# A quarter of the second chunk's projections moved beside the first's, and a rarely taken branch kept to two engines

## The chip, the core and the metric

The kernel runs on one core of a Trainium2 chip. A core has five engines with instruction streams of their own: TensorE (PE, matrix products; PEld is its loading of weights), VectorE (DVE), ScalarE (ACT), GpSimd (POOL) and SyncE (SP), which here only issues DMAs. They wait for each other through semaphores. Data is in DRAM, in the on-chip SBUF (128 partitions), and in eight PSUM banks of 128 x 512 floats, into which PE writes. The metric is the device time of one execution in microseconds (us). A number such as L325 is a line of the kernel before.

## What is computed

The reference has two independent parts, whose results are concatenated:

```python
# part A: S = 2048 rows, D = 448 columns, 16 heads of 28, one key and one value for all heads
q = (x @ wq) in heads;  k = x @ wk;  v = x @ wv
p = softmax(q k^T * 28 ** -0.5)
a = concat_heads(p v) @ wo
# part B: a filter in the frequency domain
X = rfft2(x) * (w_r + 1j * w_i)
b = irfft2(X)
out = concatenate([a, b], axis=-1)
```

All of it is in 32-bit floats. Many products are made from a high and a low part of each factor (`wqh` and `wql`, `xh` and `xl`): the high part is a rounded copy in the format that PE reads fast, the low part is the rest, and three matmuls (high x high, low x high, high x low) give the product.

The softmax is taken with a shift per query that is estimated before the scores are known: a bound from the largest entries of q and k. If the bound is too wide (over `BOUND`), a block of code computes the exact row maxima instead. With this input the block is not entered.

## The kernel before

**Projections.** q, k and v are one product of x (transposed, four chunks of 512 rows, `c`) with a weight matrix of four groups of 128 columns (`g`). The 448 inner terms are cut into four quarters (`j`), 128 rows each; the last quarter has 64 rows twice, so that high and low part of x lie over each other and two matmuls do. `proj` (L321) issues the matmuls of one group and quarter, in the order (wqh, xh), (wql, xh), (wqh, xl). For chunk 0 the loop goes over quarters outside and groups inside (L351), into four PSUM banks, so that work starts with the first data; for chunks 1 to 3 it goes over groups outside (L375), one bank after the other.

**The first loads.** `raw` (L282) takes one of eight buffers and issues a load. All the loads of x and of the weights stand in SP's queue: x quarter 0 of chunk 0, the weights' quarter 0 in two pieces (columns 0 to 127 and the rest), then x and weights of quarters 1 to 3 in turn. `split_w` (L303) makes wqh on ACT and wql on DVE; `split_x` (L310) makes xh (on DVE for chunk 0, on ACT for the others) and xl on DVE. Before that PE runs 20 products of zeros (`WARM`, L277).

**Banks.** Six PSUM banks are in a ring, `free`, and `bank()` (L224) takes the next one. The two others, tags `aux` and `po`, are used by the second DFT step of part B (`fft1_mm`) in the meantime.

**The DFTs** of part B are worked in between: `fft1_*` for the first DFT in eight parts (results `bs` stored to a DRAM tensor `t1` by SP), later `fft2_*` and `fft3_*`. The copies `bs` of part 6 and 7 are on DVE.

**The end of the projections.** From L418 on, the first query tile `qa` (called `qf` there) is put together by ACT, DVE and DMAs, the bound is computed on DVE (`bits`, L435), PE does the last DFT parts and transposes the values (L445, into `pv`), and PE issues the first four score products into banks `a, b, d, f` (L453, `first_scores`). Then all five engines load `bits` from SBUF into a register (L458) and branch on it (L459). The block inside uses PE and DVE in a loop of 64 turns and at its end has the first scores again. After it ACT copies the last DFT part (`pa7`), DVE copies `pv` to `vs`, and `keys(1)` makes the second half of the keys.

**The main stage** is a list of 256 steps (`PLAN`, L46). Each step has four scores (L783), whose exp ACT takes (L786), and 16 products with vs (L758), four for each score, issued later. Units of the DFTs (A, B, Z, F) and of the output projection (W) stand between the scores at places written in the plan. PE issues in that order, by hand; from L502 on DVE's order is the program's too. A score takes the first bank of `free` and gives it back after its exp; step 0 used the four scores that were already there. The first unit A (`fft2_a`) needs `b`, which SP loads from `t1` (L550) and DVE splits (L567, L568).

Of the kernel before, what the change touches and what calls it, by code (L numbers as in the profile page):

```python
# [10 lines left out]
F32 = mybir.dt.float32  # L11
# [45 lines left out]
def kernel(ctx: ExitStack, tc: tile.TileContext, t: dict):  # L57
# [174 lines left out]
    with tc.tile_pool(name="w1", bufs=1) as w1:  # L232
# [37 lines left out]
        with tc.tile_pool(name="x1", bufs=2) as x1:  # L270
# [6 lines left out]
            for n in WARM:  # L277
                nothing = bank()
                for _ in range(n):
                    mm(nothing[:, :256], idle[:, :128], idle, start=True, stop=True)  # L280

# [39 lines left out]
            def proj(pq, xh, xl, g, j):  # L321
                gs = slice(g * 128, (g + 1) * 128)
                parts = ((wqh, xh), (wql, xh), (wqh, xl)) if j < 3 else ((wqh, xh), (wql, xh))
                for n, (w, x) in enumerate(parts):
                    mm(pq, w[:, j, gs], x[:, j], start=(j == 0 and n == 0), stop=(j == 3 and n == 1))  # L325
# [120 lines left out]
        fft1_out(6, pb6, bound)  # L446

        d, f, a, b, e, c = free
        begin = a, b, d, f

        def first_scores():
            for n, s in enumerate(begin):
                mm(s, ka[:, :128], qf[:, n], start=True, stop=True)  # L453

        first_scores()


        rv = nc.values_load(bits.bitcast(I32)[0:1, 0:1])  # L458
        with tc.If(rv > int(np.float32(BOUND).view(np.int32))), tc.tile_pool(name="g1", bufs=1) as g1:  # L459
            k4 = g1.tile([128, S], F32, name="k4")  # L460
            nc.vector.memset(k4, 0.0)
            for i in range(4):
                nc.vector.tensor_copy(k4[32 * i:32 * i + DH], kf[0:DH])
            mz = g1.tile([128, 4, 32], F32, name="mz")
            nc.vector.memset(mz, 0.0)


            qv = qraw.rearrange("p g (b q) -> p (g b) q", q=128)
            banks = a, b
            with tc.For_i(0, 64, 1) as n:  # L470
                qs = g1.tile([128, 128], F32, name="qs")
                nc.vector.tensor_copy(qs, qv[:, bass.ds(n, 1)][:, 0])
                mx = g1.tile([128, 4, 4], F32, name="mx")
                for i in range(4):
                    r = slice(32 * i, 32 * i + 32)
                    for h in range(4):
                        ps = banks[0]
                        mm(ps, qs[r], k4[r, h * 512:(h + 1) * 512], start=True, stop=True)
                        nc.vector.tensor_reduce(mx[:, i, h:h + 1], ps, axis=AX.X, op=ALU.max)
                nc.vector.tensor_reduce(mz[:, :, DH], mx, axis=AX.X, op=ALU.max)  # L480
                pt = banks[1][:, :128]
                mm(pt, mz.rearrange("p i d -> p (i d)"), ident, start=True, stop=True)
                nc.vector.scalar_tensor_tensor(qs, qs, mask, pt, op0=ALU.mult, op1=ALU.add)
                nc.vector.tensor_copy(qv[:, bass.ds(n, 1)][:, 0], qs)
# [459 lines left out]
```

## Time and profile before

| | |
|---|---|
| time, median of 3 runs | 654.41 us (654.33 to 655.7) |
| the profiled execution: its own time | 654.11 us |
| its span, first instruction to last | 652.3 us |
| PE, ACT, DVE, POOL busy | 645.8, 555.2, 360.8, 60.0 us |
| granted TensorE clock, mean | 0.999 |
| moved by DMA | 62.40 MB, mean 96 GB/s |

How to read it: the span lies inside the execution's time, some 1.8 us of which are around it. Matmuls are pipelined and their ends are modelled, so one after the other starts well before the former's end as shown; the distance of two starts says more than the length. Rows of a timeline have the start, the length, the engine, the line, the operation, the tiles written and read, and in brackets how long the engine had been idle and what ended that. An engine with a q (DVEq, PEldq) is its sequencer, which issues the instructions.

### The profile page before, as it was taken

The numbers are of one execution on the slowest core, as the hardware profiler recorded it, in microseconds if no ns is written. First come the engines' busy times: TensorE is split into PE (matmuls) and PEld (weight loads), VectorE is DVE, ScalarE is ACT, GpSimd is POOL, SyncE is SP. The second block draws the span as 40 slices with busy tenths as digits, with TensorE's granted clock in tenths as the row PEclk, the third lists the DMA queues.
The fourth block names the chain that finished last, engine by engine and source line by source line (L and its number), as shares of the span: only waits on it lengthen the run. The fifth ranks groups of instructions, "written<-read, shape, count | busy, mean of one in ns | idle before, by whom it ended". The sixth has DMA issues, their size and how long they took to land.

```text
span 652.3 us, 11930 instructions
## 1 busy us (share of the span) xinstructions
PE 645.8 (99%) x4480; PEld 378.6 (58%) x4480; DVE 360.8 (55%) x810; ACT 555.2 (85%) x1100; POOL 60.0 (9%) x111
## 2 busy tenths in 40 slices
PE   8999999999999999999999999999999999999997
PEld 6877645545545565555546565555555565565655
DVE  5999636776788732778652511356353510356533
ACT  4554899999999977999999987899999987899991
POOL 3021401101011000100010100010010100010010
PEclk9999999999999999999999999999999999999999
DMA  8756963434354123412061403131232313140001
GB/s 263 267 150 168 256 172 86 122 86 123 105 136 136 42 52 93 115 53 58 28 160 37 110 15 92 43 100 40 70 84 66 103 31 91 44 109 16 14 30 58
DMA packets 34380, 62.40 MB, mean 96 GB/s; under 512 B 6657, under 2 KB 22674, under 8 KB 33356
## 3 DMA queue, kind: packets, MB, share of 16 engines
q1 hardware_dynamic: 30448, 49.21, 26.9%
q0 software_dynamic: 3296, 11.49, 6.8%
q8 instruction: 36, 0.59, 0.4%
q10 hardware_dynamic: 576, 0.92, 0.4%
q14 instruction: 24, 0.20, 0.1%
HBM read 29.35 MB, written 14.75 MB: 68 GB/s over the span
## 4 chain that ended last, share of the span: by engine, by line
PE 88%; ACT 0%; ACTq 0%; issue 0%
PE s L783 30%; PE s L758 22%; PE sx L758 9%; PE po L783 5%; PE po L758 4%; PE s L678 4%; PE sx L783 4%; PE s L641 2%; PE s L629 1%; PE po L678 1%; PE s L538 1%; PE s L539 1%; PE s L537 1%; PE sx L629 0%; PE sx L678 0%; ACT yb L683 0%
## 5 line engine op out<-in xcount | busy, mean ns | idle before, releaser
L786 ACT ACTIVATE p<-s 128x512 f32<-128x512 f32 x795 | 430.2, 651 | 42.1 <-PE s L783 41.0
L783 PE MATMUL s<-qa,ka 128*128 128x512 f32 x791 | 245.9, 407 | 0.0
L783 PEld LDWEIGHTS s<-qa,ka 128*128 128x128 f32 x791 | 142.7, 188 | 86.3 <-ACT p L786 50.5
L758 PE MATMUL s<-p,vs 128*32 128x512 f32 x1280 | 149.3, 596 | 0.0
L758 PEld LDWEIGHTS s<-p,vs 128*32 128x32 f32 x1280 | 36.2, 109 | 81.4 <-issue 78.9
L786 ACT ACTIVATE p<-po 128x512 f32<-128x512 f32 x124 | 80.2, 647 | 3.5 <-PE po L783 3.4
L786 ACT ACTIVATE p<-sx 128x512 f32<-128x512 f32 x105 | 69.1, 658 | 4.1 <-PE sx L783 4.0
L666 DVE RECIPROCAL r<-r 128x128 f32<-128x128 f32 x64 | 61.0, 953 | 2.3
L758 PE MATMUL sx<-p,vs 128*32 128x512 f32 x512 | 59.6, 596 | 0.0
L783 PE MATMUL po<-qa,ka 128*128 128x512 f32 x124 | 50.5, 407 | 0.0
L783 PE MATMUL sx<-qa,ka 128*128 128x512 f32 x105 | 42.0, 400 | 0.0
L685 DVE COPY ya<-s 128x448 f32<-128x448 f32 x9 | 5.6, 624 | 56.1 <-PE s L678 56.1
L649 POOL TENSOR_TENSOR yo<-y 128x226 f32<-128x226 f32 x16 | 10.0, 622 | 273.7 <-issue 248.4
L758 PEld LDWEIGHTS sx<-p,vs 128*32 128x32 f32 x512 | 14.5, 109 | 32.8 <-issue 31.4
L758 PE MATMUL po<-p,vs 128*32 128x512 f32 x256 | 29.9, 596 | 0.0
L783 PEld LDWEIGHTS po<-qa,ka 128*128 128x128 f32 x124 | 23.4, 188 | 10.8 <-ACT p L786 7.0
L643 DVE COPY m<-s 128x452 f32<-128x452 f32 x14 | 8.8, 628 | 33.8 <-PE s L641 33.8
L631 DVE COPY z<-s 113x512 f32<-113x512 f32 (+1 forms) x11 | 7.6, 691 | 35.4 <-PE s L629 30.5
L325 PE MATMUL s<-xh,wqh 128*128 128x512 f32 x64 | 26.1, 408 | 0.8 <-ACT wqh L307 0.8
L325 PE MATMUL s<-xh,wql 128*128 128x512 f32 x64 | 25.4, 397 | 0.3 <-DVE wql L308 0.2
L783 PEld LDWEIGHTS sx<-qa,ka 128*128 128x128 f32 x105 | 19.7, 188 | 8.8 <-ACT p L786 3.5
L329 ACT ACTIVATE qraw<-s 128x512 f32<-128x512 f32 x16 | 9.3, 600 | 18.0 <-PE s L325 18.0
(188 smaller groups left out, 726.6 us busy)
## 6 DMA issues: line engine op xcount, KB each, us to landing
qa<-qa SPq DMA_DIRECT2D x15, 512.0 KB
raw<-xa SPq DMA_DIRECT2D x16, 256.0 KB, 5.5
xb<-xb SPq DMA_DIRECT2D x8, 512.0 KB, 3.5
qa<-qh SPq DMA_DIRECT2D x64, 64.0 KB, 2.0
qa<-ql SPq DMA_DIRECT2D x60, 64.0 KB, 2.0
ob<-yo SPq DMA_DIRECT2D x16, 226.0 KB, 2.2
t<-bs SPq DMA_DIRECT2D x16, 225.0 KB, 3.4
wr<-wr POOLq DMA_DIRECT2D x16, 225.0 KB, 3.8
```

Source lines behind the costliest of these rows:

```text
L325: mm(pq, w[:, j, gs], x[:, j], start=(j == 0 and n == 0), stop=(j == 3 and n == 1))
L329: out = nc.scalar.activation(qraw[:, g, cs], pq, AF.Copy)
L537: mm(out, fc[w + "h"], h, start=True, stop=False)
L631: nc.vector.tensor_copy(z[:w], pz[:w].rearrange("p j (r n) -> p r j n", r=2))
L641: mm(py[:, k], z[:w, r, js], cs3[:w, k], start=True, stop=True)
L643: nc.vector.tensor_copy(m, py)
L649: nc.gpsimd.tensor_tensor(yo[:, 0:2], y1[:, 0], y1[:, 1], op=ALU.add)
L666: nc.vector.reciprocal(r, r)
L678: mm(p, x[c][:, g, s], w[:, g], start=(g == 0 and n == 0), stop=(g == NG - 1 and n == 2))
L758: mm(po[c, g][32 * i:32 * i + 32], vs[:, kc], ps[i // 2][:, i % 2], start=(kc == 0), stop=(kc == 15))
L783: begun.append(mm(sc, ka[:, kc * 128:(kc + 1) * 128], qa[c, g][:, n], start=True, stop=True))
L786: nc.scalar.activation(ps[-1][:, n % 2], sc, AF.Exp, scale=SCALE)
```

## The change

Three things are changed.

- x quarter 0 of chunk 1 is loaded third, after the weights' quarter 0 and before x quarter 1 of chunk 0. Its 12 products (four groups, three each) are issued right after those of chunk 0's quarter 0. Chunk 1's four sums are therefore open while chunk 0's are: their banks are `aux`, `po` and two of the ring, and all eight banks are in use. `parts_of(1)` comes earlier; chunk 1 later does quarters 1 to 3 only. The first load for chunk 2 is issued behind the first loads of the DFT.
- Inside `proj` the order is (wqh, xh), (wqh, xl), (wql, xh). In quarter 0 of chunk 0 the groups 1 to 3 first do the two products with wqh, all three groups, and then those with wql. Two more products of zeros stand behind group 0.
- The value load and the branch are for DVE and POOL alone, and stand ahead of the two copies `fft1_out(6, ...)`, which now come after the block. The block is written for these engines: keys are spread over the partitions by DMA through DRAM, and products and maxima are made on DVE, without loops (8 x 4 x 64 turns of three instructions each). The first four scores are no longer issued ahead of the branch: step 0 issues its own, like every other, and the ring starts as `a, b, d, e, f, c`.

```diff
@@ -274,10 +274,14 @@
             nc.vector.memset(idle, 0.0)
-            for n in WARM:
+
+            def zeros(n):
                 nothing = bank()
                 for _ in range(n):
                     mm(nothing[:, :256], idle[:, :128], idle, start=True, stop=True)
+
+            for n in WARM:
+                zeros(n)
@@ -291,6 +295,8 @@
                 nc.sync.dma_start(wr[0][:, s], t["wq"][:, 0, s])
+
+            xr[1, 0] = raw(t["xa"][1, :, 0], nc.sync)
             for j in range(1, NK):
@@ -318,11 +324,13 @@
-            def proj(pq, xh, xl, g, j):
+            def proj(pq, xh, xl, g, j, some=(0, 1, 2)):
+
                 gs = slice(g * 128, (g + 1) * 128)
-                parts = ((wqh, xh), (wql, xh), (wqh, xl)) if j < 3 else ((wqh, xh), (wql, xh))
+                parts = ((wqh, xh), (wqh, xl), (wql, xh)) if j < 3 else ((wqh, xh), (wql, xh))
                 for n, (w, x) in enumerate(parts):
-                    mm(pq, w[:, j, gs], x[:, j], start=(j == 0 and n == 0), stop=(j == 3 and n == 1))
+                    if n in some:
+                        mm(pq, w[:, j, gs], x[:, j], start=(j == 0 and n == 0), stop=(j == 3 and n == 1))
@@ -347,17 +355,31 @@
             parts_of(0)
+            parts_of(1)
             pqs = [bank() for _ in range(NG)]
+
+            pq1 = [ps_x.tile([128, 512], F32, name="pq", tag="aux"), ps_o.tile([128, 512], F32, name="po")]
             for j in range(NK):
                 split_x(*xs[0], 0, j)
                 split_w(j)
-                for g in range(NG):
-                    proj(pqs[g], *xs[0], g, j)
-                xr[1, j] = raw(t["xa"][1, :, j], nc.sync)
+                if j:
+                    for g in range(NG):
+                        proj(pqs[g], *xs[0], g, j)
+                    xr[1, j] = raw(t["xa"][1, :, j], nc.sync)
+                else:
+                    proj(pqs[0], *xs[0], 0, 0)
+                    zeros(2)
+                    pq1.extend((bank(), free[-2]))
+                    for some in ((0, 1), (2,)):
+                        for g in range(1, NG):
+                            proj(pqs[g], *xs[0], g, 0, some)
+                    split_x(*xs[1], 1, 0)
+                    for g in range(NG):
+                        proj(pq1[g], *xs[1], g, 0)
             fft1_consts()
             fft1_load(0)
-            parts_of(1)
-            for j in range(NK):
+            xr[2, 0] = raw(t["xa"][2, :, 0], nc.sync)
+            for j in range(1, NK):
                 split_x(*xs[1], 1, j)
                 xr[2, j] = raw(t["xa"][2, :, j], nc.sync)
@@ -374,8 +396,8 @@
                 for g in range(NG):
-                    pq = bank()
-                    for j in range(NK):
+                    pq = pq1[g] if c == 1 else bank()
+                    for j in range(1 if c == 1 else 0, NK):
                         proj(pq, *xs[c], g, j)
@@ -443,56 +465,46 @@
-        fft1_out(6, pb6, bound)
-
-        d, f, a, b, e, c = free
-        begin = a, b, d, f
...
-        first_scores()
-        rv = nc.values_load(bits.bitcast(I32)[0:1, 0:1])
+        rv = nc.values_load(bits.bitcast(I32)[0:1, 0:1], engines=[mybir.EngineType.DVE, mybir.EngineType.Pool])
         with tc.If(rv > int(np.float32(BOUND).view(np.int32))), tc.tile_pool(name="g1", bufs=1) as g1:
...
+            kd = dp.tile([DH, S], F32, name="kd")
+            nc.gpsimd.dma_start(kd, kf[0:DH])
+            mx = g1.tile([128, NG, 64, 8], F32, name="mx")
+            for h in range(8):
+                kb = g1.tile([128, DH, 256], F32, name="kb")
+                nc.gpsimd.dma_start(kb, kd[:, h * 256:(h + 1) * 256].unsqueeze(0).to_broadcast([128, DH, 256]))
+                for g in range(NG):
+                    for b in range(64):
...
+                        nc.vector.tensor_tensor(pr, kb, qb, op=ALU.mult)
+                        nc.vector.tensor_reduce(sm, pr.rearrange("p d k -> p k d"), axis=AX.X, op=ALU.add)
+                        nc.vector.tensor_reduce(mx[:, g, b, h:h + 1], sm, axis=AX.X, op=ALU.max)
...
-            on_act = nc.scalar.activation(bits, bits, AF.Copy)
-            first_scores()
-        behind(fft1_a_out(7, 1, pa7), on_act)
+        on_dve = fft1_out(6, pb6, on_dve)
+        fft1_a_out(7, 1, pa7)
         ev = nc.vector.tensor_copy(vs, pv)
         behind(ev, on_dve)
@@ -501,8 +513,9 @@
+    d, f, a, b, e, c = free
     free.clear()
-    free.extend((e, c))
+    free.extend((a, b, d, e, f, c))
@@ -778,11 +791,8 @@
-                if step:
-                    sc = take()
-                    begun.append(mm(sc, ka[:, kc * 128:(kc + 1) * 128], qa[c, g][:, n], start=True, stop=True))
-                else:
-                    sc = begin[n]
+                sc = take()
+                begun.append(mm(sc, ka[:, kc * 128:(kc + 1) * 128], qa[c, g][:, n], start=True, stop=True))
                 nc.scalar.activation(ps[-1][:, n % 2], sc, AF.Exp, scale=SCALE)
```

More of the change, by code (lines that the diff above doesn't have):

```diff
@@ new lines @@
+        rv = nc.values_load(bits.bitcast(I32)[0:1, 0:1], engines=[mybir.EngineType.DVE, mybir.EngineType.Pool])
+        with tc.If(rv > int(np.float32(BOUND).view(np.int32))), tc.tile_pool(name="g1", bufs=1) as g1:
+            kd = dp.tile([DH, S], F32, name="kd")
[6 more added lines that the diff above has]
+                    for b in range(64):
+                        if b % 32 == 0:
+                            qx = g1.tile([128, 1024], F32, name="qx")
+                            nc.vector.transpose(qx, qraw[:, g, b * 32:b * 32 + 1024])
+                        pr = g1.tile([128, DH, 256], F32, name="pr")
+                        sm = g1.tile([128, 256], F32, name="sm")
+                        qb = qx[:, b % 32 * 32:b % 32 * 32 + DH].unsqueeze(2).to_broadcast([128, DH, 256])
+                        nc.vector.tensor_tensor(pr, kb, qb, op=ALU.mult)
+                        nc.vector.tensor_reduce(sm, pr.rearrange("p d k -> p k d"), axis=AX.X, op=ALU.add)
+                        nc.vector.tensor_reduce(mx[:, g, b, h:h + 1], sm, axis=AX.X, op=ALU.max)
+            mz = g1.tile([128, 32, 32], F32, name="mz")
+            nc.vector.memset(mz, 0.0)
+            for g in range(NG):
+                for b in range(2):
+                    qs = qraw[:, g, b * 1024:b * 1024 + 1024]
+                    nc.vector.tensor_reduce(mz[:, :, DH], mx[:, g, b * 32:b * 32 + 32], axis=AX.X, op=ALU.max)
+                    nc.vector.transpose(qx, mz.rearrange("p b d -> p (b d)"))
+                    nc.vector.scalar_tensor_tensor(qs, qs, mask, qx, op0=ALU.mult, op1=ALU.add)
```

25 lines of the change are left out of this document (removed).

## The prediction, made before the changed kernel was built

> **What bounds the kernel now.** I read the page first, from its first and fourth parts.
>
> ```profile
> span 652.3 us, 11930 instructions
> ...
> PE 645.8 (99%) x4480; PEld 378.6 (58%) x4480; DVE 360.8 (55%) x810; ACT 555.2 (85%) x1100; POOL 60.0 (9%) x111
> ...
> PE 88%; ACT 0%; ACTq 0%; issue 0%
> ```
>
> TensorE (PE) is busy for nearly the whole span, and the chain of waits runs 88% through it. A time can only go down here where PE (or ACT, where ACT leads) stands idle, or where its work is cut. The change cuts no matmul, so I looked for the stages with idle time, in the view of busy times by window.
>
> ```profile
> 5.10:10.70 5.60, 4.55 (x17) 2.76 (x14) 2.48 (x6) 1.16 (x2) 0.00 (x0) 1.00 0.93 297
> 10.70:27.85 17.15, 17.15 (x75) 13.92 (x75) 16.64 (x29) 9.81 (x17) 2.41 (x5) 1.00 0.91 310
> ...
> 72.95:100.00 27.05, 27.05 (x162) 13.74 (x166) 11.43 (x22) 26.99 (x56) 2.90 (x6) 1.00 0.74 204
> 100.00:630.00 530.00, 530.00 (x3366) 298.76 (x3359) 278.26 (x645) 481.32 (x959) 38.05 (x68) 1.00 0.28 76
> ```
>
> The columns after the length are PE, PEld, DVE, ACT and POOL busy with instruction counts, then clock, DMA share and GB/s. Three things are seen. From 5.10 to 10.70 PE has gaps while DMA is 0.93 busy: the projections wait for data. From 10.70 on, 75 matmuls fill 17.15 us, which gives 0.229 us for each. From 72.95 to 100 ACT is busy for 26.99 of 27.05 us, so the exps lead there and the first exp's start sets the rest; later PE leads. The clock is 1.00 throughout. So two places can move the end: the stall before 10.7, and the gap ahead of the first exp at 72.95.
>
> **Start: the second chunk's first quarter.** The rows of the timeline (start, length, engine, idle time before and its releaser):
>
> ```profile
> 4.28 0.69 DVE L317 TENSOR_TENSOR xl<-raw,xh 128x512 fp32r<-128x512 f32 x1
> ...
> 6.91 0.52 ACT L307 ACTIVATE wqh<-raw 128x384 fp32r<-128x384 f32 x1 [2.60 <-DMA raw<-wq]
> 7.47 0.56 DVE L308 TENSOR_TENSOR wql<-raw,wqh 128x384 fp32r<-128x384 f32 x1 [2.30 <-ACT wqh L307]
> 7.49 0.50 PE L325 MATMUL s<-xh,wqh 128*128 128x512 f32 x1 [0.76 <-ACT wqh L307]
> 7.94 0.42 DVE L313 CAST xh<-raw 128x512 fp32r<-128x512 f32 x1
> 8.08 0.50 PE L325 MATMUL s<-xh,wql 128*128 128x512 f32 x1
> 8.40 0.69 DVE L317 TENSOR_TENSOR xl<-raw,xh 128x512 fp32r<-128x512 f32 x1
> 9.21 0.63 ACT L307 ACTIVATE wqh<-raw 128x512 fp32r<-128x512 f32 x1 [1.77 <-DMA raw<-wq]
> 9.88 0.69 DVE L308 TENSOR_TENSOR wql<-raw,wqh 128x512 fp32r<-128x512 f32 x1 [0.79 <-ACT wqh L307]
> 10.62 0.50 PE L325 MATMUL s<-xh,wql 128*128 128x512 f32 x1 [0.20 <-DVE wql L308]
> 11.22 0.63 ACT L307 ACTIVATE wqh<-raw 128x512 fp32r<-128x512 f32 x1 [1.38 <-DMA raw<-wq]
> ```
>
> Weights land at 6.91, 9.21 and 11.22, two 256 KB loads apart each time, so one load takes about 1 us of the queue. PE stops three times: for the rest of wqh at 7.49, for wql at 8.08, and for the next quarter's wql at 10.62. The matmul at 10.62 is the 14th of the projections (12 of quarter 0, then one with wqh and one with wql of quarter 1). The eleven matmuls from the 14th to the 24th take 11 x 0.229, and 0.11 more because the first after a wait is 0.50 long where others are 0.39. So the 24th is issued by 10.62 + 2.52 + 0.11 = 13.25.
>
> After the change PE does 3 matmuls of group 0, two matmuls of zeros inside the wait that ends at 7.49, then six with wqh and xh or xl (both ready), then three with wql, ready at 7.47 + 0.56 = 8.03 and so early. With the first at 7.49 these nine are through at 7.49 + 0.11 + 9 x 0.229 = 9.66. Then come the 12 of the second chunk's first quarter. Their input is now third in SP's queue, the place whose load was cast at 7.94 before; ACT's copy follows at about 7.9 and takes 0.63, DVE's subtraction 0.69, so xh is there at 8.55 and xl at 9.25, both before 9.66. The 24 matmuls are issued at 9.66 + 12 x 0.229 = 12.41. **Gain 0.84.** It needs the weights of quarter 1, pushed back by one load to about 10.2, plus 0.63 and 0.69: 11.55, before 12.41. Quarter 2 comes to 12.2 + 1.4 = 13.6, before 12.41 + 2.75. From there PE runs on without a gap as before (17.15 of 17.15 us).
>
> What costs nothing here: the zeros, hidden by the wait that ends at 7.49 (two matmuls of 256 columns, 0.23 us at the pitch above, if it were gone); the second chunk's banks held early, aux and po among them, which are first wanted again at 36.43 (the row below); the copies of chunk 0 out of PSUM, which come later, while PE has its own banks for chunk 1; the load of the weights' last quarter, ninth in SP's queue now, which waits for the buffer that DVE gives back at 4.28 + 0.69 and lands about where the ninth did; the load for chunk 2, which keeps its place behind the DFT's.
>
> ```profile
> 36.43 0.41 PE L158 MATMUL pbb<-a,fw 64*64 64x225 f32 x2
> ```
>
> Bounds: if none of the 21 matmuls from 7.49 on is held at all, 12.30 and 0.95. If DVE takes quarter 1 of chunk 0 (landed near 9.2 now) ahead of the new subtraction, xl comes at 9.2 + 0.42 + 0.69 + 0.69 = 11.0 where PE wants it at 9.9, and the 0.84 turns into a loss of 0.3. The source puts the new split first, so I take 0.84.
>
> **Branch.** The sequencers' rows for the value load (L458) and the branch (L459), and the engines around them:
>
> ```profile
> L458 DVEq TENSOR_LOAD <-bits x1: 542/542/542, 69.1 to 69.1; - x1
> L458 ACTq TENSOR_LOAD <-bits x1: 1267/1267/1267, 69.8 to 69.8; - x1
> ...
> L459 DVEq COMPARE_BRANCH  x1: 72/72/72, 69.7 to 69.7; - x1
> L459 DVEq EVENT_SEMAPHORE  x1: 21/21/21, 71.0 to 71.0; - x1
> ...
> L459 PEldq COMPARE_BRANCH  x1: 352/352/352, 72.4 to 72.4; - x1
> L459 PEldq EVENT_SEMAPHORE  x1: 51/51/51, 72.8 to 72.8; - x1
> ```
>
> ```profile
> 69.86 1.14 DVE L168 COPY bs<-s 128x450 f32<-128x450 f32 x2
> 70.07 0.55 ACT L145 ACTIVATE a<-s 128x450 f32<-128x450 f32 x1
> 71.47 1.20 PE L453 MATMUL s<-qa,ka 128*128 128x512 f32 x4
> 71.49 0.55 ACT L145 ACTIVATE a<-s 128x450 f32<-128x450 f32 x1 [0.87 <-ACTq L459]
> 71.58 0.69 DVE L496 COPY vs<-s 128x512 f32<-128x512 f32 x1 [0.57 <-PE s L445]
> 72.95 1.58 ACT L786 ACTIVATE p<-s 128x512 f32<-128x512 f32 x3 [0.91 <-PEq L459]
> ```
>
> Scores are there from 71.47 + 0.50 on, yet the first exp waits 0.91 us until PE's sequencer has loaded the value, branched and raised its semaphore at 72.8. That wait goes, and so do ACT's 0.87 and SP's share. What is late next? PE no longer branches, but its first score reads qa, which the skipped body could rewrite on DVE, so it now waits for DVE's semaphore behind the branch. DVE's sequencer reaches the branch at 69.7, ahead of its engine, since its input is out at 69.05. Behind the branch on DVE now stand the two bs copies (1.14 us, which free banks d and f for scores 2 and 4), vs, the second half of the keys, and later a store.
>
> The jump itself has no row: before, DVE's body was a short loop; now it is unrolled, 8 x 4 x 64 x 3 = 6,144 tensor instructions, to be jumped over. Instructions are brought in by DMA:
>
> ```profile
> q8 instruction: 36, 0.59, 0.4%
> q14 instruction: 24, 0.20, 0.1%
> ...
> qa<-qh SPq DMA_DIRECT2D x64, 64.0 KB, 2.0
> ...
> qa<-ql POOLq DMA_DIRECT2D x4, 64.0 KB, 4.1
> ```
>
> 0.59 MB over PE's 4480 + 4480 instructions is 66 bytes each, so the body is some 0.4 MB, about 49 packets of the q14 size (0.20 MB / 24 = 8 KB). DVE's new place can hardly have been fetched when it jumps. Low end: 0.35 us, the longest branch row. High end: 4.1 us, a DMA of this very moment on a busy queue. I take 2.0, the row of a small transfer, since 8 KB is smaller still.
>
> With 2.0, DVE is behind the jump at 69.77 + 2.0 = 71.8; the first score starts at 71.85 instead of 71.47, ends 0.50 later, and the first exp starts at 72.4 instead of 72.95: **gain 0.55** (0.93 with 0.35, where the score starts at 71.47 as before; a loss of 1.55 with 4.1). The first bs copy ends at 72.4, in time for score 2; score 3 has ACT's bank, free by 71.2; exps 0 to 3 last until 74.4, and the next scores' banks come at 72.95 and 73.65 (vs).
>
> What DVE does behind it comes later, and that is the price:
>
> ```profile
> 74.70 0.60 DVE L168 COPY bs<-po 128x450 f32<-128x450 f32 x1
> ...
> 90.41 0.40 DVE L567 CAST bh<-b 128x450 fp32r<-128x450 f32 x1 [13.41 <-DMA b<-t]
> 90.84 0.63 DVE L568 TENSOR_TENSOR b<-b,bh 128x450 fp32r<-128x450 f32 x1
> ...
> 92.78 0.37 PE L539 MATMUL po<-b,g1h 128*128 128x450 f32 x1
> ...
> SPq L550 <- DMA t<-bs: 6.6, 1, 6.6
> ```
>
> The first unit A of the second DFT stage waits for b, loaded from t1 once the last bs is stored. Before, the last bs ended at 75.30, 3.72 us after vs began at 71.58. With 2.0 it ends at 71.8 + 1.14 + 3.72 = 76.7: 1.4 later. The slack at L539 is 92.78 - 91.47 = 1.31, and PE arrives 0.55 sooner, so it can stall by 0.64. The store landed 6.6 us into SP's wait with DMA 0.74 busy, so part of the 1.4 is queueing that a later store would not meet. I take 0.2 off, ends 0 and 0.64.
>
> [...]
>
> POOL's queue: it loaded and branched before too, its body is a few DMA issues, and nothing on it stands ahead of the scores. SP loses its own load and branch and issues the last stores when DVE is ready. The order of the banks keeps its rotation, so steps from 1 on are as before.
>
> **Sum.** 0.84 + 0.55 - 0.2 = 1.2 us. Against the profiled execution's 654.11 (span 652.3, 1.8 around it) this gives 652.9; the median of the runs is 0.30 above that execution, so 653.2.
>
> **Rivals.**
> *Short jump.* Nothing has to be fetched, or it takes under 1 us. For it: DVE's, ACT's and POOL's branch rows. Against: the body's 49 packets. Gain 0.84 + 0.93 = 1.77, time 652.6.
> *Long fetch, the other side.* Place: the DVE jump. If it takes t, the first exp is at 69.77 + t + 0.63, so the branch breaks even at t = 2.55, the whole change at 3.4 without the stall of unit A, and it is slower by 0.2% (1.31 us) from about 4.5. With t = 5: 0.84 - 2.45 - 0.2 = -1.8, time 656.2. For it: PE's branch of 352 ns beside 72 on DVE, and the loaded queues (4.1). Against: small transfers at 2.0. [...]
> *Even.* t between 2.8 and 4.2, which leaves +0.6 to -0.8 less the stall: about 654.4.
> *Start does not gain.* DVE or the new load is late, as in the bound above: -0.3 + 0.55 - 0.2 = 0.05, time 654.35. For it: one queue carries all the loads at 0.93 DMA share, and DVE is behind at 7.94. Against: xl at 9.25 has 0.6 us before PE's second matmul wants it.
>
> **How the numbers follow.** Forecast (t of 1 to 2.8, start gains) 0.44, of which 0.25 passes 0.2%; short jump 0.16; even 0.16; start lost 0.07; long fetch 0.17. A run of this kernel can tell about 0.2%, 1.3 us (three runs span 654.33 to 655.7). Faster by more: 0.25 + 0.15 = 0.40. Slower by more: 0.17 and some of the even case, 0.21. Within: 0.39. The range goes from 652.3 (short jump, every bound good) to 655.9 (t near 4.8); the forecast's own is 652.6 to 653.9.
>
> **What would show it.** Right: the matmul that opens quarter 1 follows the 12 of the second chunk without a gap near 12.4; chunk 1 ends 0.8 sooner than 27.85; no row of L459 on ACT, PE or SP; the first exp near 71.6 on the span's clock (72.4 less 0.84), with PE's first score released by DVE's sequencer. The time from DVE's branch to its next instruction is t itself. Wrong: an ACT copy of the new xh behind the second weights; a DVE silence of over 3 us behind the branch; PE idle ahead of the first L537. It would also be wrong if matmuls of the main stage got slower, which nothing here lets expect.

## The result, and the profile after

Six runs of the changed kernel have a median of 657.19 us (655.98 to 659.39), six of the kernel before 654.14 (652.54 to 655.7). The ratio is 1.0051, with an interval of 1.0030 to 1.0071: about 3 us slower, where 1.2 us faster was predicted, and outside the range of 652.3 to 655.9. The profiled execution took 656.29 us, with a span of 654.5. In two of the experiments below one of twelve runs was at a granted clock of 0.66 or 0.75 (911 and 804 us), and the ratios leave it out.

The page of the changed kernel: the engines' busy times, the granted clock in 40 slices, the first line of the chain, and the group of the scores.

```profile
span 654.5 us, 11934 instructions
...
PE 646.4 (99%) x4482; PEld 379.2 (58%) x4482; DVE 360.8 (55%) x810; ACT 555.2 (85%) x1100; POOL 60.7 (9%) x111
...
PEclk9999899999999999999999999999999999999999
...
PE 88%; ACT 0%; ACTq 0%; issue 0%
...
L795 PE MATMUL s<-qa,ka 128*128 128x512 f32 x795 | 247.9, 408 | 1.8 <-DVEq L470 1.8
```

Busy times and the chain are as before. What is new is one 8 in the clock's row, in the fifth slice (65 to 82 us), and one idle time of 1.8 us ahead of a score, which ends with DVE's sequencer at L470, the branch.

The start, from the timeline of the changed kernel (start, length, engine, idle time before in brackets):

```profile
5.69 0.52 ACT L313 ACTIVATE wqh<-raw 128x384 fp32r<-128x384 f32 x1 [1.41 <-DMA raw<-wq]
...
6.55 0.47 PE L333 MATMUL s<-xh,wqh 128*128 128x512 f32 x1
...
8.71 0.39 PE L333 MATMUL pq<-xh,wqh 128*128 128x512 f32 x1
...
11.21 0.39 PE L333 MATMUL s<-xh,wql 128*128 128x512 f32 x1
11.44 0.39 PE L333 MATMUL s<-xh,wqh 128*128 128x512 f32 x1
```

The second chunk's products (tile pq) begin at 8.71, no wait stands in brackets, and the 24th product starts at 11.21. Before, the 24th of that order started at 13.03 in its profile. The fourth product, the first that needs the second piece of the weights, starts at 6.55 here and at 7.49 before, because that piece came earlier (wqh at 5.69, before at 6.91).

The branch, from the same timeline:

```profile
68.17 0.16 DVE L457 TENSOR_REDUCE bits<-s 1x1 f32<-1x16 f32 x1
...
69.64 1.18 PE L467 MATMUL s<-ident,kf 32*128 32x32 f32 x16
...
72.57 1.44 PE L795 MATMUL s<-qa,ka 128*128 128x512 f32 x4 [1.75 <-DVEq L470]
72.60 1.16 DVE L168 COPY bs<-s 128x450 f32<-128x450 f32 x2 [3.39 <-DVEq L470]
73.11 2.06 ACT L796 ACTIVATE p<-s 128x512 f32<-128x512 f32 x4 [2.71 <-PE s L795]
...
73.68 0.68 DVE L508 COPY vs<-s 128x512 f32<-128x512 f32 x1
...
75.26 1.65 PE L795 MATMUL s<-qa,ka 128*128 128x512 f32 x3
```

and the sequencers' rows at the branch (count, nanoseconds, time in the span):

```profile
L470 POOLq EVENT_SEMAPHORE  x4: 17/43/43, 70.7 to 71.2; - x4
...
L470 DVEq COMPARE_BRANCH  x1: 72/72/72, 69.0 to 69.0; - x1
L470 POOLq INC_SWDGE_SEM  x1: 618/618/618, 71.2 to 71.2; - x1
L470 DVEq EVENT_SEMAPHORE  x1: 21/21/21, 72.5 to 72.5; - x1
```

DVE branches at 69.0 and does nothing until its semaphore at 72.5: 3.4 us. PE's last work ahead of the branch, 16 small transposes, ends at 70.82; its first score can start only at 72.57. The windows around it, with the columns of the prediction's first part:

```profile
27.00:54.90 27.90, 27.07 (x421) 20.73 (x410) 27.70 (x54) 15.75 (x29) 4.01 (x8) 1.00 0.62 177
...
69.50:72.55 3.05, 1.31 (x25) 1.07 (x16) 0.00 (x0) 0.90 (x2) 0.00 (x0) 1.00 0.59 149
74.30:78.50 4.20, 4.20 (x29) 1.64 (x21) 4.01 (x8) 2.94 (x6) 3.02 (x6) 0.59 0.99 280
78.50:100.00 21.50, 21.50 (x127) 10.95 (x124) 6.09 (x11) 20.91 (x43) 0.00 (x0) 1.00 0.73 189
100.00:630.00 530.00, 530.00 (x3363) 299.19 (x3365) 280.46 (x649) 481.86 (x960) 38.05 (x68) 1.00 0.28 76
```

Right behind the gap PE is busy for all of 74.30 to 78.50, but at a granted clock of 0.59. The records of the clock show one stretch at half speed, 74.38 to 77.79, 3.41 us long. Half of it, 1.71 us, is what it would cost, by estimate, if PE led throughout. The same window before:

```profile
74.30:78.50 4.20, 4.20 (x24) 1.93 (x26) 2.57 (x5) 4.20 (x10) 2.12 (x4) 1.00 1.02 308
```

The profiled executions part at four landmarks of the timeline: the last of the 88 products of chunks 0 and 1, the bound (bits), the first exp, the 17th exp, each by its start.

| | last product | bound | first exp | 17th exp | span |
|---|---|---|---|---|---|
| before | 27.53 | 68.89 | 72.95 | 80.60 | 652.32 |
| after | 25.71 | 68.17 | 73.11 | 82.87 | 654.50 |
| gained or lost by then | -1.82 | -0.72 | +0.16 | +2.27 | +2.18 |

So 1.82 is won at the start, 1.10 of it given back by the bound, 0.88 lost between bound and first exp, 2.11 on the next 16 exps, and from there to the end both need the same time (571.72 and 571.63). The main stage is unchanged, as predicted. The runs lose more than this profile because its execution is the second shortest of six: it had a mean clock of 0.997, the other five 0.992 to 0.996. One half-speed stretch is 1.71/654.5 = 0.0026 of that mean, against the 0.999 of the kernel before's profiled execution, so the others lost what one to three such stretches would make. Where they lost it isn't known, since only the profiled execution has a record.

Where the 1.10 went shows in the waits of PE and in DVE's rows. PE's waits, changed kernel:

```profile
PE s L795 <- DVEq L470: 1.8, 1, 1.8
...
PE s L354 <- DVE qm L351: 1.0, 1, 1.0
```

The same stage before, as a window:

```profile
27.85:54.80 26.95, 26.95 (x435) 21.19 (x434) 26.66 (x53) 14.69 (x27) 4.01 (x8) 1.00 0.57 166
```

Before, PE was busy for 26.95 of 26.95 us, but so nearly was DVE: 26.66. PE comes sooner in the changed kernel, DVE does not, and at key_max (L354) PE waits 1.0 us for qm, the maximum of the queries.

### The profile page after: what moved, and what is told of

Same layout as the page of the kernel before. It is cut to its first block, busy times and chain, and to the rows that moved or that the text cites. A ratio compares the mean times of both kernels' runs of the same rounds, so it can differ in the third digit from the quotient of the medians.

```text
span 654.5 us, 11934 instructions
## 1 busy us (share of the span) xinstructions
PE 646.4 (99%) x4482; PEld 379.2 (58%) x4482; DVE 360.8 (55%) x810; ACT 555.2 (85%) x1100; POOL 60.7 (9%) x111
## 4 chain that ended last, share of the span: by engine, by line
PE 88%; ACT 0%; ACTq 0%; issue 0%
PE s L795 31%; PE s L771 22%; PE sx L771 9%; PE po L795 5%; PE po L771 4%; PE s L691 4%; PE sx L795 4%; PE s L654 2%; PE s L642 1%; PE po L691 1%; PE s L552 1%; PE s L551 1%; PE s L550 1%; PE sx L642 0%; PE sx L691 0%; ACT yb L696 0%
## 5 line engine op out<-in xcount | busy, mean ns | idle before, releaser
L795 PE MATMUL s<-qa,ka 128*128 128x512 f32 x795 | 247.9, 408 | 1.8 <-DVEq L470 1.8
L795 PEld LDWEIGHTS s<-qa,ka 128*128 128x128 f32 x795 | 143.9, 189 | 88.9 <-ACT p L796 50.3
L771 PE MATMUL s<-p,vs 128*32 128x512 f32 x1280 | 149.5, 597 | 0.0
L771 PEld LDWEIGHTS s<-p,vs 128*32 128x32 f32 x1280 | 36.2, 109 | 81.6 <-issue 78.5
L771 PE MATMUL sx<-p,vs 128*32 128x512 f32 x512 | 59.6, 596 | 0.0
L795 PE MATMUL po<-qa,ka 128*128 128x512 f32 x124 | 50.5, 407 | 0.0
L795 PE MATMUL sx<-qa,ka 128*128 128x512 f32 x105 | 42.0, 400 | 0.0
L771 PEld LDWEIGHTS sx<-p,vs 128*32 128x32 f32 x512 | 14.5, 109 | 32.8 <-issue 31.4
L771 PE MATMUL po<-p,vs 128*32 128x512 f32 x256 | 29.9, 596 | 0.0
L795 PEld LDWEIGHTS po<-qa,ka 128*128 128x128 f32 x124 | 23.4, 188 | 10.8 <-ACT p L796 7.0
L795 PEld LDWEIGHTS sx<-qa,ka 128*128 128x128 f32 x105 | 19.7, 188 | 8.8 <-ACT p L796 3.5
L568 POOL DMA_DIRECT2D wr<-wr x16 | 8.4, 533 | 163.9 <-DVE pwr L596 158.8
L333 PE MATMUL s<-xh,wqh 128*128 128x512 f32 x56 | 22.9, 410 | 0.0
```

What stands on the lines that cost most here:

```text
L568: ld = nc.gpsimd.dma_start(b2[n, q][64 * r:64 * r + 64], t[n][:, 4 * q:4 * q + 4])
L771: mm(po[c, g][32 * i:32 * i + 32], vs[:, kc], ps[i // 2][:, i % 2], start=(kc == 0), stop=(kc == 15))
L795: begun.append(mm(sc, ka[:, kc * 128:(kc + 1) * 128], qa[c, g][:, n], start=True, stop=True))
```

## The experiments

Each run below stands beside runs of the kernel before on the same chip: their medians are 653.33 us on the first (25 runs), 653.06 on the second (35), and 653.73 and 653.81 in two groups on the third (29 and 16).

### The halves, the jump and the gap

**Start alone.** The hunks of the projections, with the old branch.

```diff
+            xr[1, 0] = raw(t["xa"][1, :, 0], nc.sync)
...
-                parts = ((wqh, xh), (wql, xh), (wqh, xl)) if j < 3 else ((wqh, xh), (wql, xh))
+                parts = ((wqh, xh), (wqh, xl), (wql, xh)) if j < 3 else ((wqh, xh), (wql, xh))
...
+                    for g in range(NG):
+                        proj(pq1[g], *xs[1], g, 0)
```

> The kernel before with the changes at the start alone (the early load, the second chunk's first quarter beside the first's, wqh first); the branch as before. Theory (the long jump is at fault, the start is not): the bound is out 0.7 us sooner, as in the changed kernel (68.17 against 68.89), and the whole is 0.7 us faster than before. Rival (the loss comes from the start, by banks or loads): slower than before by 1 us or more.

Measured: 653.60 us, ratio 1.0005 (0.9994 to 1.0017): no gain in the runs, although the last product starts at 25.88 in its profile. The gain that the expectation foresaw isn't there. PE's waits show the place, though with a smaller price than in the changed kernel:

```profile
PE s L354 <- DVE qm L351: 0.2, 1, 0.2
```

**Branch alone.** The other hunks, with the old start.

```diff
-        first_scores()
-        rv = nc.values_load(bits.bitcast(I32)[0:1, 0:1])
+        rv = nc.values_load(bits.bitcast(I32)[0:1, 0:1], engines=[mybir.EngineType.DVE, mybir.EngineType.Pool])
...
-                sc = begin[n]
+                sc = take()
```

> The kernel before with the new branch and block alone, the start as before. Theory: DVE is silent for 3.4 us behind its branch, the first exp starts near 73.8, and the whole is 3.7 us slower than before (the 3.0 us of the changed kernel and the 0.7 that its start gains). Rival (the start is at fault): no slower than before.

Measured: 655.20, ratio 1.0023 (1.0008 to 1.0039). DVE is silent for 3.41 us; bound to first exp takes 4.91 (before 4.06), first to 17th exp 8.25 (before 7.65) although the clock is whole in the profiled stage. Of the eight runs five have a clock under 0.999, down to 0.995. The profiled one is among them with 0.998, but its record has no half speed at the gap, only from 651.68 to its end, when PE has nothing left to do. The three runs at 0.999 took 654.20 to 654.47, about 1 us above the median before; the five others took 655.17 to 656.61. So the branch is the part that costs: about 1 us where the clock is whole, and some 1 to 2 more in the others.

**A short block.** The changed kernel with the skipped block cut from 6,256 DVE instructions to 72.

```diff
+TURNS = 8
...
-            for h in range(8):
+            nc.vector.memset(mx, 0.0)
+            for h in range(1):
...
-                for g in range(NG):
-                    for b in range(64):
+                for g in range(1):
+                    for b in range(TURNS):
```

> The changed kernel with 8 turns in the block in place of 2,048 (the block, which is not entered with this input, no longer finds the row maxima). Theory: DVE's jump is within what is already fetched and costs under 0.3 us; the first score follows the transposes near 71.0, the first exp comes near 71.4, no half clock, and the whole is 1.6 us faster than before. Rival (what holds the first score is POOL's way round the block, which waits for its outstanding DMAs and then raises their semaphores, to 71.8): the first score stays near 72, the whole is no faster than before.

Measured: 653.36, ratio 1.0000 (0.9990 to 1.0011). From the waits of DVE and from the timeline:

```profile
DVE bs L169 <- DVEq L471: 0.5, 1, 0.5
```

```profile
69.98 1.16 DVE L169 COPY bs<-s 128x450 f32<-128x450 f32 x2 [0.49 <-DVEq L471]
...
71.02 1.20 PE L797 MATMUL s<-qa,ka 128*128 128x512 f32 x4
```

The silence falls from 3.4 to 0.5 us, the score starts as soon as PE's transposes are through, and the first exp comes 3.11 us after the bound: 0.95 less than before, where the prediction's short jump had 0.93. The whole gain of the branch depends on the length of what is skipped. POOL's share of the branch, a row INC_SWDGE_SEM of 0.618 us in the changed kernel and 0.626 here, is not what holds the score. The time as a whole still does not drop by the expected 1.6: PE waits 0.6 for qm (and 1.2 for weights at the start), the first 17 exps take 0.35 longer than before, and four of twelve runs have a clock of 0.996 to 0.998 (that of the profiled one, 0.998, again comes from its last 2 us). (The kernel before had such a clock in 2 of its 25 runs beside these.)

**Small work in the gap.** The changed kernel with 24 more transposes of 32 columns ahead of the branch, so that PE has work for the 1.75 us (they are written over).

```diff
+        for b in 24 * (0,):
+            nc.tensor.transpose(pv[:, b], kf[32:64, b * 128:(b + 1) * 128], ident[32:64, 32:64])
```

> The changed kernel with 24 more of the transposes that PE does ahead of the block (the same results again, 1.77 us by the 16 that take 1.18), so that PE is not idle while DVE's jump lasts. Theory: DVE's silence stays at 3.4 us and the first exp near 73.1, but the clock is not halved from 74.4 to 77.8, and that is worth 1 to 1.7 us: 1.3 to 2 us slower than before in place of 3. Rival (the halved clock does not come from PE's idle time, or costs nothing because ACT leads there): as the changed kernel, 3 us slower.

Measured: 656.16, ratio 1.0053 (1.0035 to 1.0072). The profiled execution keeps a clock of 0.999, but the five others have 0.992 to 0.997 as without the transposes. So the expected gain did not come, although the gap is filled in the profile (PE waits 0.2 us for DVE's sequencer). Two readings are left. The filler may be too light, or the clock may fall elsewhere: PE's wait at key_max, 1.1 us in this profile, is still there, and a case below shows a half clock behind that wait. The two fillers below that kept the clock stand in kernels without that wait, so this run doesn't tell which.

**Full work in the gap.** Branch alone, with eight score products of 512 columns ahead of the value load (written over as well).

```diff
+        for _ in range(8):
+            mm(free[2], ka[:, :128], qf[:, 0], start=True, stop=True)
```

> The new branch alone (start as before), with eight full score products of 512 columns behind the transposes whose results are written over, so that PE does full work for 1.83 us while DVE's jump lasts. Theory: DVE's silence stays 3.4 us, the first exp stays where it is with the branch alone, but no run has a granted clock under 0.998, and the median is 1 us slower than before in place of 1.9. Rival (the clock is lowered for another reason): clock and time as with the branch alone.

Measured: 654.09, ratio 1.0003 (0.9986 to 1.0021), clock 0.998 to 1.000 in all twelve runs.

```profile
70.11 2.09 PE L448 MATMUL s<-qa,ka 128*128 128x512 f32 x8
72.13 1.45 PE L776 MATMUL s<-qa,ka 128*128 128x512 f32 x4
72.16 1.16 DVE L168 COPY bs<-s 128x450 f32<-128x450 f32 x2 [3.67 <-DVEq L451]
```

DVE is silent as long as ever (3.67), and the score comes as late. The medians differ by 1.0 us, as in the runs of the branch alone that kept their clock; the part above that is gone. (The ratio is nearer to 1, perhaps because five of the 35 runs of the kernel before had a clock of 0.993 to 0.997 themselves.) So with the gap on PE the clock is under 0.999 in five of the eight runs of the branch alone, and in one of twelve (0.998) with the gap filled with whole products.

### The start's lost gain

**Less work on DVE.** In the start alone, in the changed kernel and in the kernel before, two of the eight additions and subtractions that fold each input part of the DFT (parts 0 to 5) go to GpSimd.

```diff
+            eng = nc.gpsimd if q < 6 else nc.vector
...
-                    nc.vector.tensor_tensor(y[:, 2], o2[:, 0], o2[:, 1], op=ALU.subtract),
-                    nc.vector.tensor_tensor(y[:, 3], o2[:, 0], o2[:, 1], op=ALU.add)]
+                    eng.tensor_tensor(y[:, 2], o2[:, 0], o2[:, 1], op=ALU.subtract),
+                    eng.tensor_tensor(y[:, 3], o2[:, 0], o2[:, 1], op=ALU.add)]
```

> The changes at the start alone, and two of the eight instructions of each DFT fold (parts 0 to 5) moved from DVE to POOL, which takes some 0.35 us off DVE for each of them, 4 us before the maximum of q's first columns (key_max, near 53 us). Theory (DVE is the bound between 27 and 54 us, so that what PE gains at the start ends at key_max, where PE waited 0.2 to 1.0 us for DVE's qm in the runs with the new start): that wait is gone, the bound is out 0.5 us sooner than with the start alone, and the whole is 0.5 to 1 us faster than before. Rival (PE, not DVE, sets the time of key_max): as the start alone, the same as before.

> The changed kernel with the same two instructions on POOL. Theory: PE's wait of 1.0 us at key_max is gone; since PE's idle time there and behind the branch are what lets the clock be halved, there are fewer runs with a granted clock under 0.998, and the whole is 1 to 1.5 us faster than the changed kernel: 1.5 to 2 us slower than before. Rival (the halved clock comes from the wait behind the branch alone): clock as in the changed kernel (0.992 to 0.997), 2.3 us slower than before or more.

> The kernel before with the same two instructions on POOL: what relief on DVE is worth by itself. Theory: PE waited only 0.3 us for DVE at key_max before, so the whole is 0 to 0.3 us faster. Rival (DVE is the bound all along): 1 us faster or more.

Measured: ratios 1.0006 (0.9992 to 1.0020), 1.0060 (1.0042 to 1.0078) and 1.0010 (0.9992 to 1.0027): no relief in any. The timeline of the first of the three shows why:

```profile
48.75 0.91 POOL L124 TENSOR_TENSOR f<-xb 113x256 f32<-113x256 f32 x1
48.99 0.95 DVE L122 TENSOR_TENSOR f<-xb 113x256 f32<-113x256 f32 x1
...
53.10 0.42 DVE L121 TENSOR_TENSOR f<-xb 113x256 f32<-113x256 f32 x1
```

Such an instruction on DVE takes 0.40 to 0.46 us in the start alone, where POOL does none, and the second of the two that stayed takes 0.95 to 0.96 in all six parts, beside one on POOL: little or nothing is won on DVE. The wait at key_max grows to 0.9.

**Another order on DVE.** The start alone again; the second half of the fold of DFT part 5, four instructions that nothing wants so early, goes behind the reduction that makes qm.

```diff
-                            fft1_fold(q + 2, None if q < 5 else 0)
+                            fft1_fold(q + 2, 0 if q in (3, 5) else None)
...
-                            key_max()
+                            top = key_max()
+                            for ins in fft1_fold(5, 1):
+                                behind(ins, top)
```

> The changes at the start alone, with four instructions of one DFT fold (part 5) set behind key_max's maximum in DVE's order (1.34 us ahead of PE's need less, nothing else changed). Theory (DVE's queue, full from 27 to 54 us, is what gives the start's gain back at key_max): PE's wait for qm there is gone, the bound is out 0.5 to 1 us sooner than with the start alone, and the whole is 0.5 to 1 us faster than before. Rival (the start gains nothing that would be left over): the same as before.

> The changed kernel with the same order. Theory: PE's wait of 1 us at key_max is gone and the bound comes 1 us sooner; PE's idle time behind the branch stays, and so does some of the halved clock: 1.5 to 2.3 us slower than before in place of 3. Rival (PE's wait at key_max costs nothing in the end): 3 us slower.

> The kernel before with the same order. Theory: PE waits only 0 to 0.4 us for DVE at key_max there, so the whole is 0 to 0.4 us faster than before. Rival (DVE alone sets that time): 1 us faster or more.

Measured: start 653.05 us, ratio 0.9982 (0.9969 to 0.9995); changed kernel 655.53, 1.0025 (1.0012 to 1.0037); kernel before 653.69, 1.0000 (0.9984 to 1.0017). The start with this order is faster than both kernels, though by little: its median is 0.7 us under that of the kernel before, and 0.6 if only runs with a clock of 0.999 or more are compared. DVE's rows in the changed kernel:

```profile
53.85 0.42 DVE L123 TENSOR_TENSOR f<-xb 113x256 f32<-113x256 f32 x1
54.19 0.68 DVE L338 TENSOR_REDUCE qmx<-qraw 128x1 f32<-128x512 f32 x1
54.90 0.16 DVE L351 TENSOR_REDUCE qm<-qmx 128x2 f32<-128x8 f32 x1
```

and in the start with the new order:

```profile
52.63 0.68 DVE L117 TENSOR_TENSOR xb<-f 113x512 f32<-113x512 f32 x1
53.23 0.68 DVE L338 TENSOR_REDUCE qmx<-qraw 128x1 f32<-128x512 f32 x1
53.94 0.16 DVE L351 TENSOR_REDUCE qm<-qmx 128x2 f32<-128x8 f32 x1
```

qm is there at 53.94 instead of 54.90, and PE's wait for it is gone. In the kernel before the same order gives nothing that the ratio shows. Whether the order is worth something only with the new start is open: the intervals of the two overlap, and the seven runs of the kernel before with this order that kept a clock of 0.999 or more have a median of 653.19, close to the 653.05 of the start with it. In the changed kernel the order removes about half of the loss; the clock is 0.995 to 0.997 in all twelve runs, and in the profiled one two stretches at half speed follow each other (71.14 to 77.97):

```profile
71.10:78.00 6.90, 6.01 (x28) 3.28 (x32) 5.72 (x10) 3.53 (x8) 4.95 (x9) 0.51 0.73 212
```

**All three at once.** The changed kernel with that order and with the eight products in the gap.

> The changed kernel with the new order at key_max and with eight score products (written over later) in PE's idle time behind the transposes. Theory (the loss of 3 us is the halved clock, the wait at key_max and DVE's jump with what comes late behind it, and nothing else): no run under 0.998, some 1.3 us faster than with the new order alone, 0 to 0.6 us slower than before: what is left is the jump. Rival (a further cause in the changed kernel): 1.5 us slower than before or more, with the clock whole.

Measured: 654.51, ratio 1.0004 (0.9991 to 1.0017), clock 0.999 to 1.000 in eleven of the twelve runs. With the order and the clock mended, what is left of the loss can't be told from nothing by the ratio. But five of the 16 runs of the kernel before beside it had a clock of 0.997; the other eleven have a median of 653.15, and against them some 1.3 us are left (0.9 by the means), much as in the branch alone with its gap filled. The silence of 3.4 us is still in it, and no gain of the start shows against it. By the ratios, the order was worth 0.0026 (1.0051 to 1.0025), 1.7 us, and the clock 0.0021, 1.4 us; the intervals of each pair overlap, so both sizes are rough.

### From which length the jump costs

The changed kernel with blocks of 435, 144 and 241 DVE instructions: the edit of the short block with other values of TURNS and, for the first, `for g in range(2)`.

> The changed kernel with a block of 435 instructions on DVE in place of 6,256 (it is not entered; it would not find the row maxima). Theory (a jump beyond what is fetched costs a fetch, whatever its length): DVE is silent for 3 us or more behind its branch, as with 6,256. Rival (the silence grows with the length): under 1 us, nearer to the block of 72.

> The changed kernel with a block of 144 instructions on DVE (not entered; it would not find the row maxima). [...]

> The same with 241 instructions. [...]

One profiled run each, so their times are not compared. The waits of DVE, 435 first, then 144, then 241:

```profile
DVE bs L169 <- DVEq L471: 3.4, 1, 3.4
```

```profile
DVE bs L169 <- DVEq L471: 0.5, 1, 0.5
```

```profile
DVE bs L169 <- DVEq L471: 3.5, 1, 3.5
```

So the price has two values: DVE waits 0.5 us with 72 and 144 instructions, and 3.4 to 3.5 us (3.7 in one profile) from 241 to 6,256. It does not grow with the length; the threshold lies between 144 and 241. This is what a fetch of the target would look like. The queue of instruction loads in the changed kernel, between 70.50 and 71.00, in the middle of the silence:

```profile
q14 instruction: 2, 0.02, 7.7%
```

With 241 instructions DVE branches at 71.3 and goes on at 74.9, and one such packet falls into 72.50 to 73.00; with 144 it branches at 68.8, goes on at 69.4, and there is none in between. By the packets' records, the first packet of 8 KB behind DVE's branch starts 1.6 to 1.7 us after it in eight of the nine profiles with a long block (1.9 in the ninth), and 2.4 us after it with 72 and 144 instructions, when DVE has long been at work. One also starts 1.8 us after the old branch of the kernel before. The rows don't say for which engine a packet is, so that the silence is this fetch is likely, not shown. What sets the threshold was not shown.

The run with 241 instructions shows one thing more. PE waited 2.1 us at key_max in it, and the half speed stands behind that wait, not behind the gap at the branch:

```profile
PE s L355 <- DVE qm L352: 2.1, 1, 2.1
PE s L797 <- DVEq L471: 1.8, 1, 1.8
```

```profile
53.20:56.61 3.41, 1.29 (x17) 0.88 (x10) 3.34 (x9) 1.28 (x3) 0.00 (x0) 1.00 0.72 226
56.61:60.03 3.42, 3.42 (x9) 2.63 (x9) 3.32 (x9) 0.00 (x0) 0.00 (x0) 0.50 0.33 94
```

So the gap at the branch is not the only place, and it doesn't always halve the clock. Six profiles have it unfilled (1.7 to 1.8 us): half speed follows in three (the changed kernel, the changed kernel with the new order, the block of 435) and not in the others (branch alone, changed kernel with folds on POOL, the block of 241). In all profiles the changes of the clock are whole multiples of 3.41 us apart. On that grid the wait at key_max above lies within one stretch, and so does the gap in the changed kernel (but for its first 0.15 us) and with 435 instructions; in the other four profiles the gap is split over two stretches, and only one of them was halved. That where the idle time falls decides fits these profiles but one, and was not tested.

## Why the prediction was wrong, step by step

**The start.** The steps on PE were right: no gap between the quarters, no wait for wql, the second chunk's products without a hold. From the fourth product to the 24th the changed kernel takes 4.66 us and the kernel before 5.54: 0.88 less, where 0.84 was forecast. The rest of the 1.82 between the two profiles (24th product at 11.21 against 13.03) is luck, 0.94 by which the second piece of the weights came earlier. Over all profiles the same distance is 4.63 to 4.71 in the twelve with the new start and 5.03 to 5.54 in the five with the old one. The step that failed is "From there PE runs on without a gap as before". It was read from PE's column of the window to 27.85; the next 27 us, with DVE busy for 26.66 of 26.95, were not read. PE's lead met DVE's order there, 1.0 us went at key_max, and the start alone came out at 1.0005 instead of -0.8 us. With DVE's later work moved behind qm the start was faster than before (0.9982, 1.2 us by the ratio, 0.7 by the medians).

**The branch.** This is the term of the sum that came out with the other sign: a gain of 0.55 was a loss of 0.88. The mechanism was right: ACT, PE and SP have no rows at L470, DVE's sequencer releases the first score, and t is DVE's time from its branch to its next work. The size was off: "I take 2.0, the row of a small transfer" measured 3.4. By the prediction's own formula the exp then starts at 69.77 + 3.4 + 0.63 = 73.8 on the clock of before, 0.85 later than 72.95; measured was 0.88 more between bound and first exp. With t = 0.5 the formula's 0.93 came out at 0.95. The nearest row for a jump over some 0.4 MB of instructions was not that of a transfer of a few kilobytes on its own; a value near the high end of 4.1 would have been the careful choice. The prediction had named the sign of its being wrong, a silence of DVE of over 3 us, and that is what came.

**What DVE does behind it.** No wait of the second DFT stage's first unit A shows among PE's waits, where -0.2 was taken. A price came sooner, on the first 17 exps: 0.6 us with a whole clock (branch alone, 8.25 against 7.65). DVE's lateness can be only a part of it, since 0.35 is there with the short block too (8.00), where DVE is not late; the rest of the cause was not traced.

**What was missing.** "The clock is 1.00 throughout" was read of the kernel before and carried over. The prediction had PE wait for the jump, and priced that wait only by its length. With t = 3.4 PE stands idle for 1.75 us behind small transposes, and the next stage ran at half clock for one stretch of 3.41 us in two of the six profiles with such a gap, for two in one, for none in three. In the profiles one stretch there takes the first 17 exps from 8.25 to 9.76 us, two to 10.36. With the order mended, filling the gap is worth 1.4 us by the ratios, and the runs under 0.998 fall from twelve of twelve to none of eleven: that the gap costs the clock is shown. In the changed kernel's profile 1.75 us behind 16 small transposes was enough: the half clock stands from 74.38 to 77.79. How light the work around a gap may be is not settled, since the filler of small transposes left the wait at key_max in place.

**The rivals.** The long fetch had the right sign with a chance of 0.17, but its threshold was wrong: it said slower by 0.2% only from t of about 4.5. With t = 3.4 its sum, 0.84 - 0.85 - 0.2, is a loss of 0.2, the "even" case; the clock (1.4) and DVE's order (1.7), rough as they are, make it about 3. The start that does not gain was a rival too, for another cause (late data for the new products), which did not occur.

**Open.** The start alone gives nothing in the runs, although its profile shows a lead and only 0.2 us of waiting at key_max; the start with the order is 0.7 to 1.2 faster, more than that wait. So the account of the start's lost gain is in part argued. What lowers the clock in a few runs with the block of 72 instructions and of the kernel before, where PE has no gap at the branch, was not tried; a wait at key_max is a candidate for the former (0.6 us in its profile). Nor was a complete block written as a loop, short enough to jump for nothing, together with the start and its order.

## What to carry to other kernels

Where an engine skips a block at run time, keep the block short (72 and 144 instructions on DVE cost 0.5 us of silence here, 241 and more 3.4 to 3.7; a loop in place of the unrolled body was not tried), and let TensorE's next work not hang on the engine that jumps (PE stood idle for 1.75 us). Before crediting PE with an earlier start, read the other engines' busy share over the whole stretch up to the next meeting point: an engine at 99% there can give the time back (DVE, busy for 26.66 of 26.95 us, and PE's wait of 1.0 us for qm). A wait of PE of under 2 us can cost more than its length: behind 1.75 us the clock was halved for 3.41 us in the changed kernel. With eight whole products as filler the clock was 0.998 to 1.000 in 23 of 24 runs; with 24 small transposes it was 0.992 to 0.997 in five of six. A mean clock alone doesn't say where it was lost (the 0.998 of the branch alone came from its last 2 us): read the records.

## What the runs showed of the hardware

- A taken branch on DVE over 241, 435 or 6,256 instructions silenced it for 3.4 to 3.7 us, over 72 or 144 for 0.5.
- Idle times of 1.7 to 1.8 us on PE were followed by a half clock of 3.41 us in two profiles and of 6.83 in one, and by none in three; one of 2.1 us was followed by 3.41. With 24 transposes of 32 columns in the gap, and a wait of 1.1 us elsewhere, five of six runs were at 0.992 to 0.997; with eight products of 512 columns, and no such wait, 23 of 24 were at 0.998 to 1.000.
- The clock's changes were whole multiples of 3.41 us apart in every profile.
- A two-input sum of 113x256 took DVE 0.40 to 0.46 us with none on POOL, and 0.95 beside one on POOL, itself 0.91.
- POOL, skipping a block with its own DMAs, had a row INC_SWDGE_SEM of 0.618 us at the branch (0.626 with 72, 144, 241 and 435 instructions on DVE); in the kernel before it had none.
- Matmuls with a factor of 128x512 took 0.39 to 0.41 us on the mean in the changed kernel's profile where both factors are rounded copies (L333, L795), and 0.60 where neither is (L771, with 32 columns of the other factor in place of 128); those of the start were issued 0.22 to 0.24 us apart (6.86 to 11.21).
